# Attention with forget gates, then an MLP: VectorE takes two quads' denominators ahead of other quads' transpositions beside chunk 0's second layer

## The chip, the cores and the metric

The kernel runs on one core of a Trainium2 chip. The metric is device time in microseconds (us) for one execution. The core's engines each run their own instruction stream in order: TensorE (PE, with its weight loads shown as PEld), VectorE (DVE), ScalarE (ACT), GpSimd (POOL) and SyncE (SP). They wait for one another through semaphores. DMAs are issued from the queues of SP, POOL and ACT.

## The reference

Eight batches of eight heads, 576 positions, head size 64. The result of the attention, 4608 tokens of 512 features, goes through an MLP with 2048 hidden units.

```python
scores = scale * np.matmul(q, k.transpose(0, 1, 3, 2))
cum = np.cumsum(np.log(np.clip(f, 0.0001, 1.0)), axis=-1)
decay = cum[:, :, :, None] - cum[:, :, None, :]
scores = np.where(causal, -1000000000.0, scores + decay)
attn = np.exp(scores - np.max(scores, axis=-1, keepdims=True))
attn = attn / (np.sum(attn, axis=-1, keepdims=True) + 1e-09)
x = np.matmul(attn, v)            # then heads side by side: (4608, 512)
h = x @ w_in
g = 0.5 * h * (1.0 + np.tanh(c * (h + 0.044715 * h * h * h)))
out = g @ w_out
```

## The kernel before, in words

**Tiling.** The 64 pairs of batch and head are worked in 16 *quads* of four heads: quad i holds half of the heads of batch i // 2. The MLP works in nine *chunks* of 512 tokens. Attention of later quads and the MLP of earlier chunks are interleaved on TensorE, so that it always has something to do.

**One quad.** The steps are words of a hand-written schedule:
- LK.i and LQ.i load k and q on the GpSimd queue into one of two buffers each (`k_c`, `q_c`, chosen by i % 2). LV and LX load v for a batch into one of two buffers `v_nat`.
- TK.i and TQ.i (`transpose_words`, L197, VectorE) put k and q with the head's features on the partitions, into one of two buffers `kT` and `qT`. They free `k_c` and `q_c` for the load of quad i + 2.
- VW.i (GpSimd) or vw.i (VectorE) multiplies v by the decay's weights (`make_vw`, L214), and CL.i (L219) copies a block of the result.
- S.i.r computes the scores of round r for the four heads (L261, TensorE) and their exponentials (L269, ScalarE) into `pt`. H.i.r.g does it for one pair of heads. Quads from 2 on have three rounds, 0 to 2. The scores' banks come from the pool `psS`, which has two buffers.
- M.i.r masks the diagonal blocks on GpSimd (L275), and m.i.r does it on VectorE as a product with a triangle of ones (L304).
- D.i computes the denominators: a product on TensorE (L329, with `w_bf`), then on VectorE a transposition into `den` (L348), a reciprocal (L350), and a transposition into `rb` (L352).
- V.i.x computes the output for one half x of the features: a product on TensorE (L329, with `vw`), then a multiplication by `rb` on VectorE into `xT` (L360). v.i.x is the same with a bank from `psS`.

D and V write their product into the pool `psO`, tag "po", which has one buffer. So the product of V.i.0 waits until D.i's transposition (L348) has read the buffer, and each later product waits for the VectorE instruction that reads the one before.

**Chunk 0's second layer.** F.0.n and f.0.n take n matmul steps of `mlp_out(0)` (L635, TensorE; f tiles each step into four by columns). After 16 steps VectorE copies the bank (L640) and SP stores it. The steps are spread between the words of quads 2 to 4. After them the words I.1.x (L374) begin chunk 1's first layer: 64 matmuls one after the other, which need `xT` of quads 2 and 3.

**What sets the order.** The schedule is manual. Each engine gets its instructions in the order of the words in the string FRONT (L73 to L83), and `run` (L778) plays it word by word. A gate such as `LV.3.0@LQ.7` makes a load wait for the landing of another load. Chunk 0's second layer lies in the lines of FRONT that begin with LQ.4, f.0.1 and H.4.0.1. VectorE's order there, before:

```
vw.2  TQ.4  TK.4  CL.2  D.2  (bank's copy)  V.2.0  m.3.0  TK.5  V.2.1  CL.3  m.3.1  TQ.5  D.3  V.3.1  v.3.0  (bank's copy)  CL.4
```

GpSimd's order there is LQ.5, VW.3, LK.6, M.3.2, LQ.6, LQ.7, VW.4, M.4.0, LK.7. LK.6 waits for TK.4, LQ.6 for TQ.4, LQ.7 for TQ.5 and LK.7 for TK.5, since each overwrites the buffer that the transposition reads.

Of the kernel before, what the change touches and what calls it, by code (L numbers as in the profile page):

```python
# [16 lines left out]
def kernel(  # L17
# [10 lines left out]
    nc = tc.nc  # L28

    B, H, S, D = q.shape  # L30
    BH = B * H
    NT = (S + 127) // 128
# [8 lines left out]
    NQ = BH // 4  # L41
# [25 lines left out]
    LOW, HIGH = NT, NT - 1  # L67
# [7 lines left out]
        H.1.0.0 vw.1.0 M.1.0.1 M.1.0.0 WI.3 WI.4 WI.5 D.0.0 B.2.384 H.1.1.1 V.0.0.0 H.0.1.1 V.0.1.0 H.0.1.0 D.1.0 B.1.384 V.1.0.0 M.0.1 WI.6 WI.7  # L75
        H.1.1.0 M.1.1 V.1.1.0 Q.0.3.0 vw.0.1 h.0.0.0 h.0.0.0 M.0.3 LQ.2 LK.2 Q.1.3.1 h.0.0.1 h.0.0.1 S.1.2 M.1.3 VW.1.1 WO.0 D.0.1 j.0.1 j.0.1 j.0.1
        j.0.1 E.0.0 j.0.1 V.0.1.1 V.0.0.1 D.1.1 J.0.2 WO.1 V.1.1.1 V.1.0.1 J.0.3 J.1.0 WO.2@WI.7 WO.3 J.1.1 TQ.2 LK.3 LQ.3 J.1.2 J.1.3 LX.1.0@WO.0
        LQ.4 TK.2 X F.0.6 LK.4 TK.3 S.2.0 M.2.0 LK.5 F.0.10 S.2.2 M.2.2 LX.1.1@WO.2 F.0.9 S.2.1 TQ.3 F.0.10 LV.2.0@LK.5 m.2.1 vw.2 TQ.4 TK.4 S.3.0
        f.0.1 CL.2 LQ.5 VW.3 D.2 f.0.6 S.3.1 F.0.6 V.2.0 m.3.0 S.3.2 TK.5 LK.6 M.3.2 f.0.7 V.2.1 CL.3 S.4.1 m.3.1 LQ.6 F.0.6 TQ.5 H.4.2.1 D.3
        H.4.0.1 LQ.7 VW.4 H.4.0.0 V.3.1 v.3.0 f.0.3 H.4.2.0 CL.4 I.1.0 m.4.1 U.0 LV.2.1@LQ.5 I.1.4 TQ.6 m.4.2.3 I.1.1 I.1.5 U.1 LV.3.0@LQ.7 LV.3.1  # L80
        m.4.2.2 TK.6 G.0 M.4.0 LK.7 LQ.8 LK.8 I.1.2 I.1.3 U.3 K.1.0 K.1.1 K.1.2 I.1.6 I.1.7 G.1.1.2 U.2 X F.1.16 S.5.0 f.1.26 S.5.1 D.4 M.5.0 f.1.16
        S.5.2 V.4.0 m.5.2.3 f.1.10 VW.5 V.4.1 K.1.3 CL.5 m.5.2.2 S.6.0 f.1.10 M.5.1 D.5 f.1.7 S.6.1 V.5.1 f.1.12 V.5.0 T.2 S.6.2 vw.6
    """  # L83

    HOMES = {1: 0, 3: 1, 0: 2}
# [41 lines left out]
    def many(n, shape, dtype, name):  # L127
        return [singles.tile(shape, dtype, name=f"{name}{i}") for i in range(n)]
# [10 lines left out]
    vw = many(2, [128, NT + 1, 4, D], BF16, "vw")  # L139
# [9 lines left out]
    wT = singles.tile([128, NQ, NT, 4], FP32, name="wT")  # L149
    w_bf = singles.tile([128, NQ, NT + 1, 4], BF16, name="w_bf")  # L150
# [523 lines left out]
    def zeros(which):  # L674

        todo = [(w_bf[0:64, :, LOW, :], idle[0:64, 0:BH].rearrange("p (i h) -> p i h", h=4))]
        todo += [(t_[0:64, LOW, :, :], idle[0:64, 0:256].rearrange("p (h d) -> p h d", h=4)) for t_ in vw]
        todo += [(t_[64:128, HIGH, :, :], idle[64:128, 0:512].rearrange("p (h d) -> p h d", h=H)) for t_ in v_nat]
        for n in which:
            nc.scalar.copy(*todo[n])  # L680
# [39 lines left out]
        by_columns[:] = [True] * tiled  # L720
        pull(fills.setdefault(c, seven_products(c) if c else mlp_out(c)), n)

    def cast_w(copy):
        copy(w_bf[:, :, 0:NT, :], wT)
        copy(w_bf[64:128, :, LOW, :], wT[0:64, :, 0, :])

    def load_values(b, half):
        return load_v(b, 4 * half, 4)

    ops = {  # L730
        "W": lambda: cast_w(nc.vector.tensor_copy),
        "w": lambda: cast_w(nc.scalar.copy),
        "Z": lambda *which: zeros(which),
        "CU": within_tiles,
        "CW": make_w,
# [119 lines left out]
```

## Time and profile before

| | before |
|---|---|
| median of three runs | 321.27 us (321.11 to 323.5) |
| the profiled execution | 321.83 us |
| its span | 320.1 us |
| TensorE busy | 314.1 us (98%) |
| VectorE busy | 252.4 us (79%) |
| ScalarE busy | 208.5 us (65%) |
| GpSimd busy | 112.8 us (35%) |

The span runs from the first to the last instruction in the trace. Busy time counts an engine's own instructions without its waits. Matmuls overlap, and their ends are modelled, so a busy TensorE isn't one at its peak. The timeline merges an engine's neighbouring instructions of the same kind into one row: start, length, engine, line, what is written from what, number, and in brackets the idle time before it with the one that ended it. Buffer numbers are left out there, so which quad a row belongs to follows from the order of the words. Single starts that the text names (such as the matmul at 59.93) are from the same trace, instruction by instruction.

### The profile page before, as it was taken

Reading aid. Unit: us, or ns where it says so; the run is one execution under the profiler, and the core shown is the slowest. Engines: PE = TensorE matmul, PEld = TensorE weight load, DVE = VectorE, ACT = ScalarE, POOL = GpSimd, SP = SyncE. Lnnn points to the kernel's source line nnn. Section 1 sums busy time; section 2 is a strip of 40 time slices with the busy share of each in tenths; the row PEclk is TensorE's granted clock in tenths of the full one; section 3 lists DMA queues with packets and bytes.
Section 4 is the critical chain, followed back from the end, with each engine's and each line's share of the span. In section 5 each row is a group of like instructions: output and inputs, shape, how many; then the busy total and the mean of one; then the engine's idle time right before and its main releaser. Section 6 shows DMA issues by size and latency. Waiting matters only on the chain.

```text
span 320.1 us, 12371 instructions
## 1 busy us (share of the span) xinstructions
PE 314.1 (98%) x5545; PEld 219.4 (69%) x5545; DVE 252.4 (79%) x398; ACT 208.5 (65%) x265; POOL 112.8 (35%) x160
## 2 busy tenths in 40 slices
PE   8999999999999999999999999999999999999995
PEld 3467744545776477766777677768766798788784
DVE  5876049986789899779987898689868969886882
ACT  5895686776766785759756865778567844722730
POOL 8897465730500219601770068204710240000000
PEclk9999999999999999999999999999999999999999
DMA  7999999898204830791159512971120112002013
GB/s 128 237 149 205 207 236 249 147 186 178 59 4 123 146 63 31 142 224 35 39 98 197 107 37 69 195 137 37 37 68 0 37 36 68 3 34 100 0 35 98
DMA packets 47573, 33.45 MB, mean 104 GB/s; under 512 B 29856, under 2 KB 42272, under 8 KB 47520
## 3 DMA queue, kind: packets, MB, share of 16 engines
q0 software_dynamic: 9712, 15.99, 29.0%
q1 hardware_dynamic: 37664, 16.60, 20.0%
q8 instruction: 43, 0.70, 1.0%
q14 instruction: 10, 0.08, 0.1%
q10 hardware_dynamic: 144, 0.07, 0.1%
HBM read 36.85 MB, written 9.44 MB: 145 GB/s over the span
## 4 chain that ended last, share of the span: by engine, by line
PE 92%; DVE 4%; DMA 1%; ACT 1%; issue 1%; DVEq 0%
PE ps_w L565 30%; PE ps_h L374 16%; PE po L329 9%; PE ps_s L261 9%; PE ps_cd L433 8%; PE ps_ab L433 6%; PE ps_h L491 4%; PE pso L635 2%; PE ps_h L388 2%; PE po_m L315 2%; PE idle_ps L239 1%; DMA gsum<-in_f_dram 1%; DVE pt L304 1%; DVE qT L197 1%; DVE kT L197 1%
## 5 line engine op out<-in xcount | busy, mean ns | idle before, releaser
L269 ACT ACTIVATE pt<-ps_s 128x1024 bf16<-128x1024 f32 (+2 forms) x98 | 92.3, 992 | 35.9 <-PE ps_s L261 32.4
L275 POOL TENSOR_SCALAR_AFFINE_SELECT pt<-pt 128x512 bf16<-128x512 bf16 (+2 forms) x67 | 39.8, 605 | 103.8 <-ACT pt L269 102.7
L374 PE MATMUL ps_h<-xT,w_in_sb 128*128 128x512 bf16 x240 | 55.1, 379 | 0.0
L565 PEld LDWEIGHTS <-gT 128*32 128x32 bf16 (+1 forms) x1247 | 50.6, 97 | 6.0 <-issue 1.7
L565 PE MATMUL ps_w<-w_out_sb,gT 128*32 128x256 bf16 (+1 forms) x1050 | 46.9, 273 | 0.0
L381 ACT ACTIVATE gT<-ps_h 128x1024 bf16<-128x1024 f32 x30 | 30.6, 1021 | 17.2 <-PE ps_h L374 16.7
L565 PEld LDWEIGHTS <-gsum 128*32 128x32 bf16 (+1 forms) x1256 | 39.2, 97 | 1.4
L374 PEld LDWEIGHTS <-w_in_sb 128*128 128x128 bf16 x240 | 23.4, 98 | 24.3 <-issue 0.4
L261 PE MATMUL ps_s<-qT,kT 32*128 32x448 bf16 (+5 forms) x880 | 35.7, 263 | 0.5 <-ACT pt L269 0.5
L214 POOL TENSOR_TENSOR vw<-v_nat,wT 128x1280 bf16<-128x1280 f32 (+1 forms) x13 | 29.8, 2292 | 4.4 <-DMA v_nat<-in_v_dram 3.9
L565 PE MATMUL ps_w<-usum,gsum 128*32 128x256 bf16 (+1 forms) x832 | 30.6, 273 | 0.0
L197 DVE STREAM_TRANSPOSE kT<-k_c 128x576 f32<-128x576 f32 x16 | 19.9, 1244 | 11.8 <-DMA k_c<-in_k_dram 11.8
L261 PEld LDWEIGHTS <-kT 32*128 32x128 bf16 x896 | 16.3, 93 | 17.6 <-issue 12.1
L442 ACT ACTIVATE gT<-snap 128x512 bf16<-128x512 f32 x45 | 26.1, 624 | 3.0 <-DVE snap L456 2.4
L590 DVE TENSOR_TENSOR o_st<-ps_w,snap 128x512 f32<-128x512 f32 x31 | 21.3, 686 | 8.4 <-PE ps_w L565 7.2
L433 PEld LDWEIGHTS <-w_in_sb 128*128 128x128 bf16 x240 | 23.4, 98 | 6.2 <-issue 1.5
L329 PE MATMUL po<-pt,vw 128*32 128x64 bf16 (+4 forms) x624 | 22.5, 278 | 0.4 <-DVE den L348 0.3
L329 PEld LDWEIGHTS <-vw 128*32 128x32 bf16 x672 | 14.5, 97 | 10.6 <-issue 4.4
L360 DVE TENSOR_TENSOR xT<-po,rb 128x576 bf16<-128x576 f32 x26 | 19.5, 750 | 2.9 <-PE po L329 2.2
L433 PEld LDWEIGHTS <-xT 128*128 128x128 bf16 x180 | 17.6, 98 | 5.2
L197 DVE STREAM_TRANSPOSE qT<-q_c 128x576 f32<-128x576 f32 x16 | 19.9, 1242 | 0.4 <-DMA q_c<-in_q_dram 0.4
L191 POOL DMA_DIRECT2D k_c<-in_k_dram x16 | 9.2, 578 | 25.0 <-DVE qT L197 21.0
(111 smaller groups left out, 488.3 us busy)
## 6 DMA issues: line engine op xcount, KB each, us to landing
out_dram<-o_st SPq DMA_DIRECT2D x35, 256.0 KB, 2.3
k_c<-in_k_dram POOLq DMA_DIRECT2D x16, 288.0 KB, 6.5
q_c<-in_q_dram POOLq DMA_DIRECT2D x16, 288.0 KB, 6.2
v_nat<-in_v_dram SPq DMA_DIRECT2D x16, 256.0 KB, 6.9
v_nat<-in_v_dram SPq DMA_DIRECT2D x20, 128.0 KB, 5.1
w_in_sb<-in_moe_w_in_dram POOLq DMA_DIRECT2D x8, 256.0 KB, 6.9
w_out_sb<-in_moe_w_out_dram POOLq DMA_DIRECT2D x4, 512.0 KB, 9.9
v_nat<-in_v_dram POOLq DMA_DIRECT2D x9, 128.0 KB, 6.0
```

The lines of the kernel that those rows point to most:

```text
L197: nc.vector.transpose(out=dst.rearrange("p s c -> p (s c)").bitcast(FP32) .rearrange("p (t a) -> p a t", a=S // 32), in_=src.rearrange("p ...
L214: eng.tensor_mul(vw[i % 2][:, t0:t1], vb[:, t0:t1, h0:h0 + 4, :], wT[:, i, t0:t1, :].unsqueeze(3).to_broadcast([128, t1 - t0, 4, D]))
L261: nc.tensor.matmul(tiles[h // 2][:, h % 2, c0:c0 + nq], key_columns(i, key, h, c), qq[32 * h:32 * h + 32, q0:q0 + nq, c], start=(c == 0 an ...
L269: nc.scalar.activation(p[:, 2 * g:2 * g + 2, off:off + n], t[:, :, 0:n], AF.Exp, scale=scale)
L275: nc.gpsimd.affine_select(out=x, in_=x, compare_op=ALU.is_ge, fill=0.0, base=0, pattern=pattern, channel_multiplier=-1)
L329: nc.tensor.matmul(po[r0:r0 + w.shape[-1], 448 + q0:448 + q0 + nq], w, p[:, h, col:col + nq], start=(key in (0, "low")), stop=(key in ("lo ...
L374: nc.tensor.matmul(ph[:, j, :], w_in_sb[:, dt, 128 * ft:128 * ft + 128], xT[:, dt, CH * c:CH * (c + 1)], start=(dt == 0), stop=(dt == N_DT ...
L381: nc.scalar.activation(gT[:, 2 * pr:2 * pr + 2, :], ph, AF.Gelu_apprx_tanh)
L433: nc.tensor.matmul(ps[:, j], w[:, dt, 128 * j:128 * j + 128], x[:, dt], start=(first and j == 0 and dt == 0), stop=(dt == 1), skip_group_c ...
L442: nc.scalar.activation(gT[:, ft:ft + 2, HC * j:HC * (j + 1)], x, AF.Gelu_apprx_tanh)
L565: nc.tensor.matmul(ps[c0:c0 + width, n, cols[0]:cols[1]], x[:, j, 128 * n + c0:128 * n + c0 + width], w[:, j, cols[0]:cols[1]], start=(fir ...
L590: nc.vector.tensor_add(st, ps, kept[name])
```

## The change

Four transpositions move in the string FRONT. TQ.4 goes behind D.2, TK.4 behind V.2.0, TK.5 ahead of m.3.0, and TQ.5 behind v.3.0, with LQ.7 behind it. `cast_w` gets an optional part, which no word uses.

```diff
-  ... vw.2 TQ.4 TK.4 S.3.0 f.0.1 CL.2 LQ.5 VW.3 D.2 f.0.6 S.3.1 F.0.6 V.2.0 m.3.0 S.3.2 TK.5 LK.6 M.3.2 f.0.7 V.2.1 CL.3 S.4.1
-  m.3.1 LQ.6 F.0.6 TQ.5 H.4.2.1 D.3 H.4.0.1 LQ.7 VW.4 H.4.0.0 V.3.1 v.3.0 f.0.3 H.4.2.0 CL.4 I.1.0 ...
+  ... vw.2 S.3.0 f.0.1 CL.2 LQ.5 VW.3 D.2 TQ.4 f.0.6 S.3.1 F.0.6 V.2.0 TK.4 S.3.2 TK.5 m.3.0 LK.6 M.3.2 f.0.7 V.2.1 CL.3 S.4.1
+  m.3.1 LQ.6 F.0.6 H.4.2.1 D.3 H.4.0.1 VW.4 H.4.0.0 V.3.1 v.3.0 TQ.5 LQ.7 f.0.3 H.4.2.0 CL.4 I.1.0 ...
-    def cast_w(copy):
-        copy(w_bf[:, :, 0:NT, :], wT)
-        copy(w_bf[64:128, :, LOW, :], wT[0:64, :, 0, :])
+    def cast_w(copy, rest=None):
+        i0, i1 = {None: (0, NQ), 0: (0, 2), 1: (2, NQ)}[rest]
+        copy(w_bf[:, i0:i1, 0:NT, :], wT[:, i0:i1])
+        if i1 > 2:
+            copy(w_bf[64:128, i0:i1, LOW, :], wT[0:64, i0:i1, 0, :])
...
-        "W": lambda: cast_w(nc.vector.tensor_copy),
-        "w": lambda: cast_w(nc.scalar.copy),
+        "W": lambda *rest: cast_w(nc.vector.tensor_copy, *rest),
+        "w": lambda *rest: cast_w(nc.scalar.copy, *rest),
```

VectorE's order there, after:

```
vw.2  CL.2  D.2  TQ.4  (bank's copy)  V.2.0  TK.4  TK.5  m.3.0  V.2.1  CL.3  m.3.1  D.3  V.3.1  v.3.0  TQ.5  (bank's copy)  CL.4
```

GpSimd's order, after: LQ.5, VW.3, LK.6, M.3.2, LQ.6, VW.4, LQ.7, M.4.0, LK.7.

## The prediction, made before the changed kernel ran

> **What bounds the kernel now.** I read the page first, for the chain that ended last, then that chain in order of time around chunk 0's second layer, then the busy time in windows, and at the end the timelines of VectorE, TensorE and GpSimd there. The span is 320.1 us and TensorE's clock was granted in full throughout. The page gives the chain by engine:
>
> ```profile
> PE 92%; DVE 4%; DMA 1%; ACT 1%; issue 1%; DVEq 0%
> ```
>
> Almost everything is TensorE; what an edit on VectorE can win lies in the 4%. In order of time (start, length, what) the chain leaves TensorE once in this region, from 47.6 to 61.7 us, and goes down VectorE's queue. The two transpositions TQ.4 and TK.4 (L197) stand ahead of quad 2's denominators (L348), and TK.5 and TQ.5 ahead of quad 3's:
>
> ```profile
> 49.98 1.25 DVE qT L197
> 51.23 1.09 DVE kT L197
> ...
> 52.59 0.80 DVE den L348
> ...
> 55.73 1.65 DVE pt L304
> 57.38 1.17 DVE kT L197
> ...
> 59.88 1.17 DVE qT L197
> 61.05 0.60 DVE den L348
> 61.65 0.04 issue
> 61.69 0.87 PE po L329 x24
> ```
>
> But a chain by releasers doesn't say how much TensorE lost. The windows (stretch, then busy time of PE, PEld, DVE, ACT, POOL) do:
>
> ```profile
> 48.00:64.00 16.00, 15.59 (x334) 7.92 (x334) 15.63 (x22) 10.71 (x11) 10.07 (x12) 1.00 0.95 198
> ```
>
> In these 16 us VectorE is busy 15.63 and TensorE 15.59. VectorE is saturated, and TensorE idles 0.41 us: that is about all there is to be won. TensorE's timeline shows most of it, ahead of V.2.0:
>
> ```profile
> 51.68 1.47 PE L635 MATMUL pso<-w_out_sb,gT 128*128 128x512 bf16 x6
> 53.43 0.87 PE L329 MATMUL po<-pt,vw 128*32 128x512 bf16 x24 [0.28 <-DVE den L348]
> ...
> 57.67 1.47 PE L635 MATMUL pso<-w_out_sb,gT 128*128 128x512 bf16 x6
> 59.07 0.63 PE L261 MATMUL ps_s<-qT,kT 32*128 32x320 bf16 x8
> ```
>
> The same six matmuls F.0.6 take 1.40 us from start to next start where nothing waits (57.67 to 59.07) and 1.75 where V.2.0 follows (51.68 to 53.43). V.2.0 writes the one "po" buffer, which the denominators' transposition reads until 53.38. So the stall is **0.35 us**.
>
> **The change, part by part.** No instruction is added or removed: the optional argument of `cast_w` is used by no word. On VectorE four transpositions change places with their neighbours, and one GpSimd load falls behind a product. Only waits can change.
>
> *D.2 ahead of TQ.4 and TK.4.* The product vw.2 ends at 50.06 and D.2's matmuls (49.03 to 49.71) are long done, so with CL.2 (0.22) in between the den transposition begins at 50.35 instead of 52.59 and ends at 51.13. TensorE is ready for V.2.0 at 53.08: the stall goes, -0.35, with 1.9 us to spare. rb is done at 52.25, then comes TQ.4 (1.24) to 53.4, the copy of F.0.6's bank (0.65) to 54.0, and V.2.0's multiplication (0.74), released by TensorE at about 53.9, to 54.7.
>
> *What is late next: TK.4, now behind that multiplication.* It runs from 54.6 to 55.85; before, it ended at 52.31. Its reader S.4.1 starts at 57.10, with the gain 56.75. Its cover is 0.9 us; without it every us goes straight to TensorE. TQ.4 ends at 53.4 and has 3.3 us. TK.4 and TK.5 now lie beside GpSimd's product VW.3 (54.77 to 57.10), which no transposition did before in this stage. Bounds from rows: chunk 1 has two transpositions beside the same kind of product, at their common length,
>
> ```profile
> 120.71 1.25 DVE L197 STREAM_TRANSPOSE kT<-k_c 128x576 f32<-128x576 f32 x1
> ...
> 120.86 2.33 POOL L214 TENSOR_TENSOR vw<-v_nat,wT 128x1280 bf16<-128x1280 f32 x1
> ...
> 121.81 1.24 DVE L197 STREAM_TRANSPOSE qT<-q_c 128x576 f32<-128x576 f32 x1
> ```
>
> so 0; the other end is what m.3.0 lost beside VW.3, 1.73 against 0.43 us. I take 0, the row of the very operation.
>
> *TK.5 ahead of m.3.0.* In the timeline of all engines, VW.3 and then the two mask products m.3.0 and m.3.1:
>
> ```profile
> 54.77 2.33 POOL L214 TENSOR_TENSOR vw<-v_nat,wT 128x1280 bf16<-128x1280 f32 x1 [3.94 <-DMA v_nat<-in_v_dram]
> ...
> 55.65 1.73 DVE L304 TENSOR_TENSOR pt<-pt,causal 128x512 bf16<-128x512 bf16 x1
> ...
> 59.45 0.43 DVE L304 TENSOR_TENSOR pt<-pt,causal 128x512 bf16<-128x512 bf16 x1
> ```
>
> m.3.0 stood still until GpSimd let go at 57.10 and ended 0.28 later. With TK.5 first (55.75 to 57.0), the lost 1.3 us are filled with a transposition, and m.3.0 ends at about 57.4 all the same. V.2.1's multiplication follows at 57.35 to 58.1 (before 58.40 to 59.13), CL.3, then m.3.1. D.3 needs both masks. Before, D.3's part that needs m.3.1 started at 59.93, 0.05 after m.3.1 ended (59.88), so the mask held it by about 0.05 us; I don't count that, because H.4.0.0's scores behind it start at 60.87, 0.05 after an exponential that frees their bank (59.80 to 60.82), and would wait there instead. With the change the mask is done at 58.8 and wanted at 59.55.
>
> *D.3 ahead of TQ.5.* Before, den waited for TQ.5 and ended at 61.63, and V.3.1 began 0.05 later. The last score matmul ahead of V.3.1 streamed to 61.40. D.3 began 0.09 us after such an end (59.53 to 59.62), so V.3.1 could have begun at 61.49 and lost **0.20 us**. With the change D.3 ends at about 60.15 on TensorE, den runs 60.2 to 60.95, and V.3.1 is ready at 61.1: gone. I.1.0, which needs V.3.0's multiplication and its bank (64.28 before, I.1.0 at 64.38), gets them at about 63.5 and asks at 63.8.
>
> *The queues that words are moved past.* GpSimd: LQ.7 waits for TQ.5, now after V.3.0's multiplication (63.5 to 64.7), so it issues at 64.7 instead of 61.35 and VW.4 no longer waits behind it: VW.4 starts when LQ.6's issue ends, at 59.4 instead of 61.90. Behind LQ.7 stand M.4.0 (64.19 before, now 65.3; wanted by D.4 at about 84), LK.7, LQ.8, LK.8 (wanted from 106 us on). LK.6 and LQ.6 wait for TK.4 and TQ.4, which end at 55.85 and 53.4, but GpSimd is in VW.3 until 57.10 and in M.3.2 until 58.89: nothing. SP: LV.3.0 waits for LQ.7's landing (64.9 to 66.2 before, about 4.9 us after issue, so now 69.6), but SP issued its first load only at 70.45; wanted at 99.1. The store of f.0.3 is 0.5 us later, with no reader. VectorE then runs some 0.5 to 1 us later into its next idle time (1.55 us at 71.05, waiting for ACT): hidden.
>
> Sum: -0.35 - 0.20 = **-0.55 us**, by estimates from these rows. From 64.4 us on the chain stays on TensorE, so the shift should last to the end. The profiled run took 321.83 us (span 320.1, 1.7 around it), so it would take 321.3; from the median of 321.27 I get **320.7 us**.
>
> **The rivals.**
>
> *No gain (321.3).* The stalls go but reappear a little later, as waits for ACT: scores already waited for it twice, 0.5 us in all. For it: H.4.0.0 stands right behind ACT, as told above. Against: ACT itself waits for TensorE ahead of S.4.1 (0.88 us idle), so it moves forward with it.
>
> *m.3.1 is shut out by VW.4 (slower).* VW.4 moves from 61.90 to 59.4, towards m.3.1. If m.3.1 isn't started by then, it stands until VW.4 ends (59.4 + 2.34 = 61.74) and is done 0.28 later, at 62.0; D.3 wants it at 59.55. TensorE loses 2.45, less the 0.35 won before: 321.27 + 2.1 = 323.4. It decides at m.3.1's start, which I put at 58.4, or 58.9 if one of M.3.2's selections (0.62 each) holds it first: 0.5 us short of the point at worst. The m.3.0 row is what such a wait looks like. The Trainium skill's page "SBUF — State Buffer", section "Who interferes with whom", says that a VectorE instruction with two SBUF inputs and a GpSimd one that reads SBUF hold a port pair in turn, for the whole instruction, whichever issues first. By that rule this rival is real and the order of issue alone decides; the trace agrees at m.3.0 (1.73 against 0.43).
>
> *TK.4 late for S.4.1 (slower).* If transpositions are held by VW.3 after all, TK.4 ends at 58.3 and S.4.1 loses 1.55, less 0.35: 322.5. The rows at 120.71 and 121.81 speak against it.
>
> *No moved wait at all* is excluded: VectorE runs its instructions in the written order, and the order is fixed by hand.
>
> **How the numbers follow.** Forecast (-0.55): 0.74. No gain: 0.13. m.3.1 shut out: 0.06. TK.4 late: 0.05. Unforeseen: 0.02. The three runs of before lie from 321.11 to 323.5, so 1% (3.2 us) is about what a measurement of this kernel can tell from no change. All named cases lie within it. Faster by over 1%, below 318.1, would need six times my sum: 0.01. Slower by over 1% (above 324.5) takes both slower rivals or a bad one: 0.03. The range starts at 320.0 (the windows' 0.41 us of idle counts only whole gaps; twice my sum is the most that I can find) and reaches to 322.4, over no gain and nearly to the late TK.4.
>
> **What would show it.** Right: den of quad 2 at 50.3 us and no idle time ahead of V.2.0 (52.7 to 53.1); TK.5 beside VW.3 at 1.24 us and m.3.0 near 0.4; den of quad 3 at 60.2; VW.4 at 59.4; I.1.0 at 63.8 instead of 64.38; TensorE idle under 0.1 us in 48 to 64. Wrong: a wait of S.4.1 for kT, a mask product of 1 us or more ahead of D.3, scores waiting for ACT near 60.5, or I.1.0 at 64.3 or later.

## The result, and the profile after

The changed kernel is slower: 324.39 us, median of 20 runs, against 321.76 us of 20 runs of the kernel before. The ratio is 1.0066, with a 95% interval from 1.0046 to 1.0086. This ratio and those below leave out runs more than 1.5% above the same kernel's fastest, here three of after's, from 326.66 us up; the medians' plain quotient is 1.0082. After's runs spread from 321.44 to 327.79, those of before from 320.73 to 323.5. The profiled execution took 324.76 us, its span 323.1.

The windows of after show the loss in one place (stretch, busy time of PE, PEld, DVE, ACT and POOL with instructions, the granted share of TensorE's clock, the DMA share, GB/s):

```profile
48.00:64.00 16.00, 13.14 (x262) 6.28 (x260) 14.93 (x17) 9.78 (x11) 9.51 (x10) 0.95 0.85 187
58.00:62.00 4.00, 1.46 (x33) 0.78 (x32) 3.48 (x2) 1.70 (x2) 3.20 (x3) 1.00 0.93 138
62.00:66.00 4.00, 4.00 (x88) 2.03 (x80) 2.59 (x4) 1.94 (x2) 0.00 (x0) 0.57 0.10 19
```

TensorE had 15.59 us of work in the first stretch before and has 13.14 now. From 58 to 62 it works 1.46 of 4 us (3.87 before), and in the four after that the clock is granted at 0.57. TensorE's timeline of after says what it waits for:

```profile
58.05 0.62 PE L261 MATMUL ps_s<-qT,kT 32*128 32x320 bf16 x8
58.60 0.43 PE L329 MATMUL po<-pt,w_bf 128*32 128x512 bf16 x8
61.57 0.61 PE L329 MATMUL po<-pt,w_bf 128*1 128x448 bf16 x16 [2.54 <-DVE pt L304]
62.11 1.33 PE L261 MATMUL ps_s<-qT,kT 32*128 32x64 bf16 x24
63.37 1.53 PE L329 MATMUL po<-pt,vw 128*32 128x512 bf16 x24
64.69 1.44 PE L329 MATMUL ps_o<-pt,vw 128*32 128x512 bf16 x24
```

D.3 stands 2.54 us, within its own product, for a mask product (L304). V.3.1 and v.3.0 behind it take 1.53 and 1.44 us instead of 0.87 each. VectorE and GpSimd in the same timeline:

```profile
54.00 2.33 DVE L197 STREAM_TRANSPOSE kT<-k_c 128x576 f32<-128x576 f32 x2
54.24 2.34 POOL L214 TENSOR_TENSOR vw<-v_nat,wT 128x1280 bf16<-128x1280 f32 x1 [3.69 <-DMA v_nat<-in_v_dram]
...
56.18 0.68 DVE L304 TENSOR_TENSOR pt<-pt,causal 128x512 bf16<-128x512 bf16 x1
...
57.13 1.24 POOL L275 TENSOR_SCALAR_AFFINE_SELECT pt<-pt 128x512 bf16<-128x512 bf16 x2
57.56 0.90 DVE L219 COPY vw<-vw 64x256 bf16<-64x256 bf16 x1
...
58.31 0.55 POOL L191 DMA_DIRECT2D q_c<-in_q_dram  x1
58.49 3.03 DVE L304 TENSOR_TENSOR pt<-pt,causal 128x512 bf16<-128x512 bf16 x1
...
58.88 2.34 POOL L214 TENSOR_TENSOR vw<-v_nat,wT 128x1280 bf16<-128x1280 f32 x1
```

The row of 58.49 is m.3.1. It takes 3.03 us instead of 0.43 and ends at 61.52, 0.30 after VW.4. VW.4 now starts at 58.88, since LQ.7 no longer stands ahead of it. TK.4 and TK.5 (54.00, two in 2.33) run beside VW.3 undisturbed.

From trace to trace the stage can be compared by its length, from the start of S.3.1 to the start of I.1.0, whatever came earlier: 51.11 to 64.38 before, 13.26 us; 50.44 to 67.27 after, 16.83 us. The loss of 3.57 is the sum of its parts, in starts of TensorE's groups: V.2.0 no longer waits, -0.35; D.3, 3.51 instead of 0.85, +2.66; V.3.1 and v.3.0, 2.59 instead of 1.36, +1.23; the rest +0.03. The span grew by 3.0 only, mostly because this execution came to the stage 0.67 us earlier.

### The profile page after: what moved, and what is told of

Same layout as the page of the kernel before. It is cut to its first block, busy times and chain, and to the rows that moved or that the text cites. A ratio compares the mean times of both kernels' runs of the same rounds, so it can differ in the third digit from the quotient of the medians.

```text
span 323.1 us, 12349 instructions
## 1 busy us (share of the span) xinstructions
PE 312.2 (97%) x5525; PEld 218.7 (68%) x5545; DVE 254.5 (79%) x398; ACT 208.5 (65%) x265; POOL 113.2 (35%) x160
## 4 chain that ended last, share of the span: by engine, by line
PE 83%; DMA 8%; DVE 3%; POOL 2%; ACT 2%; issue 1%; DVEq 0%; POOLq 0%
PE ps_w L565 30%; PE ps_h L374 16%; PE po L329 9%; PE ps_cd L433 8%; PE ps_s L261 8%; PE ps_ab L433 6%; DMA w_out_sb<-in_moe_w_out_dram 4%; DMA w_in_sb<-in_moe_w_in_dram 3%; PE pso L635 3%; PE ps_h L388 2%; DMA q_c<-in_q_dram 2%; ACT pt L269 1%; DVE pt L304 1%; POOL w_in_sb L180 1%; DVE kT L197 1%
## 5 line engine op out<-in xcount | busy, mean ns | idle before, releaser
L261 PE MATMUL ps_s<-qT,kT 32*128 32x448 bf16 (+5 forms) x880 | 35.0, 263 | 1.9 <-DVE qT L197 1.0
L433 PE MATMUL ps_cd<-xT 128*128 128x256 bf16 x120 | 18.0, 273 | 0.0
```

Source lines behind the costliest of these rows:

```text
L261: nc.tensor.matmul(tiles[h // 2][:, h % 2, c0:c0 + nq], key_columns(i, key, h, c), qq[32 * h:32 * h + 32, q0:q0 + nq, c], start=(c == 0 an ...
L433: nc.tensor.matmul(ps[:, j], w[:, dt, 128 * j:128 * j + 128], x[:, dt], start=(first and j == 0 and dt == 0), stop=(dt == 1), skip_group_c ...
```

## The experiments

**Theory A:** VW.4, moved ahead by the loss of LQ.7 before it, shuts m.3.1 out; D.3 waits, and the wait costs TensorE its clock. **Rival B:** the new places of the transpositions, or the late LQ.7, cost it whatever VW.4 does. Each ratio is to the kernel before.

**e1, VW.4 put back behind M.4.0**, VectorE's order as changed:

```diff
- D.3 H.4.0.1 VW.4 H.4.0.0 V.3.1 v.3.0 TQ.5 LQ.7 f.0.3 ... G.0 M.4.0 LK.7
+ D.3 H.4.0.1 H.4.0.0 V.3.1 v.3.0 M.4.0 VW.4 TQ.5 LQ.7 f.0.3 ... G.0 LK.7
```

> The changed kernel with GpSimd's VW.4 put behind M.4.0 (M.4.0 waits for the exponentials of H.4.0, so VW.4 starts at about 62.5 us instead of 58.9); VectorE's new order stays. Theory A (m.3.1 was shut out by VW.4, and TensorE's clock fell after the wait): m.3.1 takes 0.4 to 0.5 us, D.3 doesn't wait, the clock stays at 1.00, and the time is that of before less the 0.55 us of the prediction: a ratio to before of 0.998 (0.996 to 1.000). Rival B (the moved transpositions or the late load LQ.7 cost it, whatever VW.4 does): the ratio stays at 1.006 to 1.009.

Measured: 321.78 us, ratio 0.9994 (0.9977 to 1.0012). The loss is gone with this edit alone, against B. The stage took 13.48 us, and the gain of the prediction wasn't there either. The timeline of e1 shows why:

```profile
55.80 2.33 POOL L214 TENSOR_TENSOR vw<-v_nat,wT 128x1280 bf16<-128x1280 f32 x1 [4.57 <-DMA v_nat<-in_v_dram]
...
57.11 1.30 DVE L304 TENSOR_TENSOR pt<-pt,causal 128x512 bf16<-128x512 bf16 x1
...
59.11 0.89 DVE L219 COPY vw<-vw 64x256 bf16<-64x256 bf16 x1
...
59.86 0.55 POOL L191 DMA_DIRECT2D q_c<-in_q_dram  x1
60.03 0.43 DVE L304 TENSOR_TENSOR pt<-pt,causal 128x512 bf16<-128x512 bf16 x1
60.51 0.61 PE L329 MATMUL po<-pt,w_bf 128*1 128x448 bf16 x16 [0.55 <-DVE pt L304]
```

Here v landed late and VW.3 started at 55.80 (54.24 in after). So m.3.0 stood behind VW.3 (1.30 us) and CL.3 behind M.3.2's selection (0.89). m.3.1 itself ran freely beside the issue of LQ.6, but late: D.3 waited 0.55 us.

**e2, m.3.1 and CL.3 taken ahead of V.2.1's multiplication**, VW.4 early:

```diff
- m.3.0 LK.6 M.3.2 f.0.7 V.2.1 CL.3 S.4.1 m.3.1 LQ.6
+ m.3.0 m.3.1 CL.3 LK.6 M.3.2 f.0.7 V.2.1 S.4.1 LQ.6
```

> The changed kernel with the mask product m.3.1 and the copy CL.3 taken ahead of V.2.1's multiplication on VectorE, where GpSimd is still in VW.3 or M.3.2; VW.4 stays early. Theory A: m.3.1 ends by 57.5 us, before VW.4 starts at 58.9, so nothing shuts it out: ratio to before 0.998 (0.996 to 1.000), clock 1.00. V.2.1's multiplication comes some 0.6 us later, at 57.4 to 58.1, just in time for D.3 at 58.6; if that is too tight, up to 0.3 us are lost. Rival B: ratio 1.006 to 1.009.

Measured: a miss. The ratio of 1.0026 (0.9989 to 1.0063) holds for its four quickest runs alone. The other eight took 326.3 to 327.8 us, and the median of all twelve is 326.74. In the profiled run, one of the four (322.5 us), the two mask products took 2.66 us behind VW.3 and M.3.2, V.2.1's multiplication came at 59.65, and D.3 waited 1.29 us for its buffer. The shut-out only moved to an instruction with more behind it. What the runs near 327 did wasn't seen in a profile and stays open; their mean clocks are 0.983 to 0.995, that of the profiled run 0.998.

**e3, LK.6 behind M.3.2**, so that GpSimd only issues loads when m.3.1 comes:

```diff
- m.3.0 LK.6 M.3.2 f.0.7
+ m.3.0 M.3.2 LK.6 f.0.7
```

> The changed kernel with the load LK.6 put behind M.3.2, so that GpSimd runs M.3.2, then issues LK.6 and LQ.6 (57.8 to 58.95 us), then VW.4. CL.3 and m.3.1 then come to VectorE's head while GpSimd only issues loads. If the issue of a load leaves the port free (A1), m.3.1 takes 0.43 us at about 58.0 and the ratio is 0.998. If the issue holds it as well (A2), m.3.1 waits from 58.0 to 59.0 and then either runs (ratio 0.998 to 1.000) or loses to VW.4 again (ratio 1.006).

Measured: 320.59 us, ratio 0.9984 (0.9957 to 1.0012). The runs fall in groups: seven of ten at 320.3 to 320.7, one at 322.0, two at 324.0. One of the two at 324.0 is the profiled one:

```profile
58.40 0.60 POOL L191 DMA_DIRECT2D k_c<-in_k_dram  x1
58.65 0.22 DVE L219 COPY vw<-vw 64x256 bf16<-64x256 bf16 x1
58.90 3.29 DVE L304 TENSOR_TENSOR pt<-pt,causal 128x512 bf16<-128x512 bf16 x1
58.99 0.55 POOL L191 DMA_DIRECT2D q_c<-in_q_dram  x1
...
59.53 2.36 POOL L214 TENSOR_TENSOR vw<-v_nat,wT 128x1280 bf16<-128x1280 f32 x1
```

m.3.1 had 0.63 us before VW.4's recorded start, needs 0.43, and still lost. GpSimd's queue is the same in all ten runs, so by their times the mask product gets through in most of them; no profile shows one of those.

**e4, the kernel before with VW.4 ahead of LQ.7**, no transposition moved:

```diff
- H.4.0.1 LQ.7 VW.4 H.4.0.0
+ H.4.0.1 VW.4 LQ.7 H.4.0.0
```

> The kernel before with one edit: on GpSimd VW.4 goes ahead of LQ.7, so that it starts at 59.4 us instead of 61.9. VectorE's order is that of before, where m.3.1 starts at 59.45. Theory A: m.3.1 comes 0.05 us after VW.4 and is shut out until 61.7; D.3 waits 2 us: ratio 1.005 to 1.008 with no transposition moved at all. If m.3.1 slips in ahead of it: 1.000. Rival B: 1.000.

Measured: 325.71 us, four runs, ratio 1.0111 (1.0067 to 1.0155), no less than the whole change costs. Its timeline:

```profile
58.94 0.55 POOL L191 DMA_DIRECT2D q_c<-in_q_dram  x1
59.28 2.66 DVE L219 COPY vw<-vw 64x256 bf16<-64x256 bf16 x1
59.51 2.34 POOL L214 TENSOR_TENSOR vw<-v_nat,wT 128x1280 bf16<-128x1280 f32 x1
...
61.98 0.43 DVE L304 TENSOR_TENSOR pt<-pt,causal 128x512 bf16<-128x512 bf16 x1
...
62.45 0.61 PE L329 MATMUL po<-pt,w_bf 128*1 128x448 bf16 x16 [1.77 <-DVE pt L304]
```

CL.3 came first and stood 2.66 us, behind the issue of LQ.6 and VW.4, with m.3.1 queued behind it; D.3 waited 1.77 us, and the clock fell to half. This is the loss without any of the moved transpositions.

**e5, e1 and e3 together.**

> e1 and e3 together: VW.4 behind M.4.0, and LK.6 behind M.3.2, so that between VW.3 and M.3.2 and between M.3.2 and VW.4 no mask product can be shut out for more than a selection. Theory A: all runs lie where the eight undisturbed runs of e3 lay (320.3 to 320.7 us), none near 324: ratio to before 0.9965 (0.995 to 0.998), D.3 waits under 0.2 us. Rival (e3 was quicker for another reason than a free port): a spread as in e1, ratio 0.999 to 1.001.

Measured: 320.88 us, ratio 0.997 (0.9951 to 0.9989): quicker than both kernels. None of the twelve runs is near 324: eight lie at 320.6 to 320.9, close to e3's seven at 320.3 to 320.7 (seven, not eight as the expectation has it), one at 321.6, three at 322.1 to 322.3. The stage took 12.77 us, 0.49 less than before. Its timeline:

```profile
57.51 0.59 POOL L191 DMA_DIRECT2D k_c<-in_k_dram  x1
57.76 0.22 DVE L219 COPY vw<-vw 64x256 bf16<-64x256 bf16 x1
58.01 0.43 DVE L304 TENSOR_TENSOR pt<-pt,causal 128x512 bf16<-128x512 bf16 x1
58.10 0.55 POOL L191 DMA_DIRECT2D q_c<-in_q_dram  x1
...
59.73 0.78 DVE L348 STREAM_TRANSPOSE den<-po 128x576 f32<-128x576 f32 x1 [1.29 <-PE po L329]
```

CL.3 and m.3.1 come as long after LK.6's start as in e3 (0.25 and 0.50 us) and take 0.22 and 0.43. The difference between the two traces is what stands behind LQ.6 in GpSimd's queue: a product there, a word that waits here (M.4.0, for 3.70 us). By the runs' times a product there shuts m.3.1 out in some executions, not in all.

**e6, the first part alone:** D.2 ahead of TQ.4 and TK.4, nothing else.

```diff
- vw.2 TQ.4 TK.4 S.3.0 f.0.1 CL.2 LQ.5 VW.3 D.2 f.0.6 S.3.1 F.0.6 V.2.0 m.3.0 S.3.2 TK.5
+ vw.2 S.3.0 f.0.1 CL.2 LQ.5 VW.3 D.2 TQ.4 f.0.6 S.3.1 F.0.6 V.2.0 TK.4 m.3.0 S.3.2 TK.5
```

> The kernel before with the first part of the change alone: D.2 ahead of TQ.4 and TK.4, TK.4 behind V.2.0's multiplication and ahead of m.3.0; TK.5 and TQ.5 where they were, GpSimd's queue untouched. By the prediction's first step V.2.0's wait of 0.35 us goes: ratio 0.999 (0.997 to 1.000). If VW.3 shuts out m.3.0 as before and m.3.0 with it delays V.2.1's multiplication and m.3.1: up to 1.002.

Measured: 321.61 us against 322.0, ratio 0.9984 (0.9961 to 1.0006). The stage took 12.77 us, as in e5. V.3.1's wait went as well, though TQ.5 still stood ahead of D.3: D.3 started on TensorE at 60.12, and TQ.5 (59.67, 1.25) was just over when it ended (60.92 against 60.98). But v came early in this execution: VW.3 started 2.71 us after the stage's start (54.67), 3.65 in before, and TQ.5 ended 8.96 us after it instead of 9.94. So this part of the gain goes with v's landing and isn't shown to be the edit's.

**e7, TQ.5, LQ.7 and VW.4 put back**, the rest of the change kept:

```diff
- F.0.6 H.4.2.1 D.3 H.4.0.1 VW.4 H.4.0.0 V.3.1 v.3.0 TQ.5 LQ.7 f.0.3
+ F.0.6 TQ.5 H.4.2.1 D.3 H.4.0.1 LQ.7 VW.4 H.4.0.0 V.3.1 v.3.0 f.0.3
```

> The changed kernel with TQ.5, LQ.7 and VW.4 put back (TQ.5 ahead of D.3, LQ.7 ahead of VW.4). The transpositions TQ.4, TK.4 and TK.5 keep their new places. Theory A: LQ.7 waits for TQ.5, which stands behind m.3.1 on VectorE, so VW.4 can't come ahead of m.3.1: no shut-out, ratio 0.999 (0.997 to 1.000), the clock stays. Rival B: 1.006.

Measured: 321.89 us, ratio 1.0003 (0.9976 to 1.0029): no loss, so the new places of TQ.4, TK.4 and TK.5 don't cost it, though the ratio lies just above the expected range. The stage took 13.19 us: m.3.0 stood 1.59 us, and D.3 and V.3.1 waited 0.2 and 0.3.

**e8, matmuls in place of the wait.** The changed kernel, with 11 matmuls of zeros ahead of the part of D.3 that needs m.3.1 (key 1):

```diff
+            if key == 1 and fill:
+                ps_f = psM.tile([128, 512], FP32, name="ps_f", tag="m")
+                for _ in range(fill):
+                    nc.tensor.matmul(ps_f, idle[:, 0:128], idle, start=True, stop=True)
```

> The changed kernel with 11 matmuls of zeros (11 x 0.216 = 2.4 us) put into D.3's product just where it waits for m.3.1; they add nothing to the result. They take the place of the wait where m.3.1 is shut out (2.5 us in the profile of after), and add 2.4 us where it isn't. Theory (the clock falls because TensorE idles): the clock stays at 1.00 in the stage in every run and V.3.1 takes 0.68 us, not 1.33: 323.3 to 324.3 us in all runs, none above 325. Rival (the clock falls for another reason, say at fixed times or by GpSimd's load): runs with a clock of 0.995 and less remain, and the time lies at 324 to 328.

Measured: 324.62 us, ratio 1.0077 (1.0054 to 1.0101), runs from 323.31 to 326.05. The times were wider than expected, with three of ten runs above 325, and the kernel isn't quicker than after as a whole: 2.4 us of zeros were added to every run, shut out or not. Why a run at full clock took 326.05 no profile shows. The clock held: nine of ten runs show 0.999 or 1.000 and one 0.995, where thirteen of after's twenty show 0.995 or less. (Of the 35 runs of the kernel before that were measured beside e8, eight do.) Its windows have it at full in the stage:

```profile
58.00:62.00 4.00, 3.86 (x43) 1.67 (x41) 3.43 (x2) 1.56 (x2) 2.89 (x3) 1.00 0.85 134
62.00:66.00 4.00, 3.98 (x104) 2.25 (x94) 3.65 (x6) 1.96 (x3) 0.00 (x0) 1.00 0.05 10
```

VectorE was shut out in this run as well (CL.3 took 3.75 us), and v.3.0 took 0.68 us instead of 1.27. The stage took 15.57 us, 1.26 less than in after, close to the clock's share of 1.23.

**e9, VW.4 in two instructions** (`VW.4.0 VW.4.1` for `VW.4`), otherwise as changed:

> The changed kernel with VW.4 as two instructions, 512 and 768 of its 1280 elements a partition. If GpSimd gives the port up between two of its instructions (F1), a mask product that comes during the first part runs after it: D.3 waits some 1.0 us instead of 2.5, the clock stays, ratio to before 1.000 to 1.002. If a VectorE instruction that waits isn't served between two GpSimd instructions in a row (F2), m.3.1 stands for both parts as before: D.3 waits 2.5 us or a little more, ratio 1.006 to 1.010.

Measured: 326.59 us, four runs, ratio 1.0162 (1.0126 to 1.0198), F2 and worse. Its timeline:

```profile
58.43 1.24 POOL L275 TENSOR_SCALAR_AFFINE_SELECT pt<-pt 128x512 bf16<-128x512 bf16 x2
58.86 3.89 DVE L219 COPY vw<-vw 64x256 bf16<-64x256 bf16 x1
...
59.61 0.55 POOL L191 DMA_DIRECT2D q_c<-in_q_dram  x1
...
60.18 2.48 POOL L214 TENSOR_TENSOR vw<-v_nat,wT 128x512 bf16<-128x512 f32 x2
62.78 0.43 DVE L304 TENSOR_TENSOR pt<-pt,causal 128x512 bf16<-128x512 bf16 x1
```

The copy CL.3, 0.22 us of work, stood through the second selection, a load and both parts. It wasn't served at any of the three borders between them, and m.3.1 stood behind it. In after the same copy came at the same place, 0.43 us behind the start of M.3.2 (57.13 and 57.56 there, 58.43 and 58.86 here), and was served while LQ.6 was issued. So the recorded times don't tell when the issue of a load lets VectorE in.

## Why the prediction was wrong

The forecast was 320.7 us, in a range from 320.0 to 322.4; the measured median is 324.39.

**Right: V.2.0's wait.** It went, -0.35, as worked out. So did the order of the transpositions: TK.4 and TK.5 beside VW.3 took their usual time, and S.4.1 never waited for kT.

**Right in sum, open in part: V.3.1's 0.20.** With no shut-out the stage gains 0.49 us (e5) where 0.55 was forecast. But e6, where v came early, gains as much without D.3's part, while in e7, with TQ.5 ahead of D.3 as well, V.3.1 waited 0.28. So what the move of TQ.5, which set VW.4 free, is worth by itself stays open.

**Wrong: the point from which "m.3.1 is shut out by VW.4" decides.** The mechanism was named as a rival, with its place and price, and given 0.06. The step that failed is "0.5 us short of the point at worst": it took VW.4's start in the trace as the latest time for m.3.1. m.3.1 came 0.39 us before VW.4 in after and 0.63 before it in e3, and lost both times. So the margin was put nearly right, and the point that it was measured to was wrong. Where GpSimd had work right behind the issue of a load, a VectorE instruction of this kind was served in some traces (m.3.0 in before, CL.3 in after) and shut out in others (m.3.1 in after and e3, CL.3 in e4 and e9). Where GpSimd's queue waited behind the load, CL.3 and m.3.1 got through in every trace (before, e1, e5, e6, e7). Before the change that gap was LQ.7, waiting 1.97 us for TQ.5 on VectorE itself, ahead of VW.4:

```profile
58.83 0.55 POOL L191 DMA_DIRECT2D q_c<-in_q_dram  x1
61.35 0.53 POOL L191 DMA_DIRECT2D q_c<-in_q_dram  x1 [1.97 <-DVE qT L197]
61.90 2.35 POOL L214 TENSOR_TENSOR vw<-v_nat,wT 128x1280 bf16<-128x1280 f32 x1
```

The change took it away. With it put back the loss goes (e1, e5, e7), and taking it away alone makes the loss (e4).

**Mis-sized: the rival's price.** It was 2.1 us, 2.45 for D.3's wait less the 0.35. In the profiled run D.3 took 2.66 us longer, but the fall of the clock, 1.23, was left out. Not every run lost the clock: after's six runs at 1.000 have a median of 323.6, near the rival's 323.4, and its thirteen at 0.995 or less one of 325.2.

**Also left out: when v lands.** VW.3 waits for a DMA and started between 53.5 and 55.8 us in these traces. What it holds up (m.3.0, then V.2.1 and m.3.1) changes from trace to trace. The prediction laid one execution's times end to end and took margins of a few tenths for safe.

## What to carry to other kernels

When an instruction moves, ask what its wait kept apart. A wait in one engine's queue can be the gap in which another engine gets its turn, and a move on VectorE can close it through GpSimd's queue. Where two engines contend, a margin in recorded start times isn't enough: put a wait that is there in any case between them, as M.4.0's is in e5. A stall of TensorE should be priced with the clock that it may cost.

## What the runs showed of the hardware

**Waiting isn't first come, first served.** CL.3 stood through four GpSimd instructions in e9, and GpSimd's recorded start isn't the point that decides (m.3.1 came 0.63 us before it in e3). Beside the issue of a load with a waiting word behind it both run freely (e5: 0.22 and 0.43). The runs show the waiting alone; what is held, and by which rule it changes hands, no run here tells. The Trainium skill's page "SBUF — State Buffer", section "Who interferes with whom", says that whichever of the two issues first has the port pair for its whole instruction. The traces agree on the whole instruction and differ on the order: the one first by the trace lost.

**Less than one step of idling can cost the clock, and where it lies matters.** The trace's record of the clock runs in steps of 3.413 us in each kernel (58.027 us at full in after, up to 62.48, is 17 of them), and half rate in the stage lasted one step. With the steps laid through the stage, TensorE's idle time in one step was 2.50 us in after, 2.71 in e9 and 1.77 in e4, and each time the next step ran at half. In e3 a wait of 2.12 us fell across a border, 1.21 and 0.91 us, and the clock stayed:

```profile
58.00:62.00 4.00, 2.12 (x21) 0.86 (x21) 3.94 (x3) 2.80 (x3) 3.90 (x4) 1.00 0.58 93
62.00:66.00 4.00, 3.74 (x100) 2.15 (x99) 3.11 (x6) 1.94 (x2) 0.00 (x0) 1.00 0.35 66
```

Idle time in a step isn't the whole rule, though. At the kernel's end e3 and e8 have steps with 1.89 and 1.87 us idle, and the step behind them stayed at full; near its start e1 has one with 1.51 us idle (7.42 to 10.84), and the step behind it ran at half. What else counts no run here tells.

The Trainium skill's page "TensorE: Matmul & The Clock Gate", section "What's actually happening", gives a free-running window of 3413 ns, which the steps bear out. Its section "Why this matters for your kernels" advises against gaps over about 3 us; here 1.77 us within one step was enough.
